# Narrowing w_out one block behind gate and val, and turning the second part of q two slots later, in a one-core attention and gated FFN kernel

## The chip, the cores and the metric

The kernel runs on one core of one Trainium2 chip. The metric is the device time of that core in microseconds. Before the change it is 303.82 us, the median of 10 runs that lie between 303.35 and 304.21 us. All times below are microseconds unless marked otherwise; the clock granted to TensorE is 1.0 over the whole span.

## What is computed

The reference is a linear attention with sketched features, followed by a gated feed-forward layer. Cut to what matters (B=4, H=4, S=1088, D=32, r=8, F=64; 4352 tokens, model width 128, inner width 1536):

```python
def phi(x):                      # S1, S2: (8, 32)
    a = einsum('rd,bhsd->bhsr', S1, x)
    b = einsum('rd,bhsd->bhsr', S2, x)
    return einsum('bhsi,bhsj->bhsij', a, b).reshape(..., 64)
kv  = einsum('bhsf,bhsd->bhfd', phi(k), v)
z   = sum(phi(k), axis=2)
x   = (phi(q) @ kv) / (phi(q) @ z + 1e-6)      # -> (4352, 128)
out = (sigmoid(x @ w_gate) * (x @ w_val)) @ w_out
```

S1, S2 and the three weight matrices arrive as 64-bit words. The kernel reads them as pairs of 32-bit integers and makes float32 of them itself; it calls that narrowing.

## The kernel before, in words

**The feed-forward part.** The 4352 tokens are cut into nine chunks of at most 512. For a chunk, the inner width is taken in 12 blocks j of 128. One *slot* (line 395) is one such block: `w1` (line 345) issues the gate and the val matmul of block j into a PSUM tile "wave" (128x512 each, line 357), ScalarE takes the sigmoid (line 365), and in the next slot VectorE multiplies the two (`glu`, line 381, tile g). Two slots after its `w1`, `w2` (line 314) multiplies g by block j of w_out and accumulates into the PSUM tile "moeout". So slot k issues glu(k-1), w2(k-2), w1(k), in this order. One float32 matmul of 512 columns shows in the trace as two instructions of about 0.43 us each, so a slot is six of these, 2.57 us of TensorE.

**The attention part.** Tokens of batch 0 must be ready before the first slot can run. The kernel makes the first 512 tokens (q part 0) in the prologue and starts slots at once; the other 576 tokens of batch 0 (q part 1) are made while the 12 slots of chunk 0 run. That goes in these steps: `turn_q(0, 1)` transposes q part 1 on VectorE (line 436); `q01` (line 1020) projects it on TensorE (tile cqps, line 602), ScalarE copies the result to SBUF (tile cq, line 610) and issues its DMA to DRAM (dq, line 620), and SyncE loads it back, spread over the partitions, with one DMA into qp and two into bq (line 627); `qmult(0, 1)` (line 655) multiplies qp by bq on VectorE; after that the denominators and numerators of q part 1 are matmuls (dps, line 841, and nps, line 861), and the division gives the tokens. qp of q part 1 is what dps reads. The SBUF buffer of bq is the one that held k and q of batch 0 and will hold those of batch 1, so `load_kq(1)` waits for `qmult(0, 1)`.

**The order around the change.** The program order of TensorE, VectorE, ScalarE and GpSimd is the order in which the Python code issues instructions; nothing reorders it. Before the change the order is: slot 0; slot 1; `turn_q(0, 1)`; slot 2; `q01`; slots 3 to 8; `qmult(0, 1)`; `load_kq(1)`; slot 9; then slot 10 with dps and nps in front of its matmuls; slot 11 with the last product; then chunk 1.

**Narrowing.** `narrow` (line 83) is a generator. Its step 0 clips the high words on GpSimd (cap, line 97) and scales the low words on ScalarE (tail, line 101); step 1 is two VectorE operations on the high words (head, lines 105 and 109); step 2 is a square on ScalarE (line 117), put in a PSUM bank or in place in SBUF, and an add on GpSimd (line 118); step 3 is the VectorE operation that writes the float32 weights to w_sb (line 127). The first two blocks are narrowed in three parts of 256 columns each (`narrow_01`): gate and val of block 0, gate and val of block 1, and w_out of blocks 0 and 1 together. Every later block j is one part of 384 columns: gate, val and w_out of the same j (`narrow_w`). The steps of these parts are issued inside `w1` of chunk 0, after the sigmoid (lines 366 to 376), a few slots ahead of their use. The weight loads are DMAs on SyncE's queue (lines 155 and 168), issued in the prologue in the order of their blocks.

Of the kernel before, what the change touches and what calls it, by code (L numbers as in the profile page):

```python
# [8 lines left out]
F32 = mybir.dt.float32  # L9
I32 = mybir.dt.int32  # L10
# [10 lines left out]
def kernel(  # L21
# [30 lines left out]
    const = ctx.enter_context(tc.tile_pool(name="const", bufs=1))  # L52
    ld = ctx.enter_context(tc.tile_pool(name="ld", bufs=1))
    sbA = ctx.enter_context(tc.tile_pool(name="sbA", bufs=2))
    raw = ctx.enter_context(tc.tile_pool(name="raw", bufs=NJ // 2))
    sbN = ctx.enter_context(tc.tile_pool(name="sbN", bufs=1))
    sbG = ctx.enter_context(tc.tile_pool(name="sbG", bufs=6))

# [24 lines left out]
    def narrow(out, bits, eng, bank=None, copies=None):  # L83

        p, n, m = bits.shape[:3]
        lo, hi = bits[:, :, :, 0].bitcast(U32), bits[:, :, :, 1]

        def tmp(dt, tag, bufs):
            return sbN.tile([P, 3, P], dt, tag=tag, name=tag, bufs=bufs)[:p, :n, :m]

        cap, tail = tmp(I32, "cap", 6), tmp(I32, "tail", 5)
        eng.tensor_scalar(  # L97
            out=cap.bitcast(F32), in0=hi.bitcast(F32), scalar1=122880.0, scalar2=-122880.0,
            op0=ALU.min, op1=ALU.max,
        )  # L100
        nc.scalar.activation(out=tail, in_=lo, func=ACTF.Copy, scale=2.0**-29)  # L101
        yield

        head = tmp(I32, "head", 3)
        nc.vector.tensor_scalar(
            out=head, in0=cap, scalar1=3, scalar2=0x3FFFFFF8,
            op0=ALU.logical_shift_left, op1=ALU.bitwise_and,
        )
        nc.vector.scalar_tensor_tensor(  # L109
            out=head, in0=cap, scalar=-0x40000000, in1=head, op0=ALU.bitwise_and, op1=ALU.bitwise_or  # L110
        )
        yield
        square = cap.bitcast(F32)
        if bank:
            square = pso.tile([P, 512], F32, tag=bank, name="square")[:, : n * m]
            square = square.rearrange("p (n m) -> p n m", n=n)
        nc.scalar.activation(out=square, in_=cap.bitcast(F32), func=ACTF.Square)  # L117
        nc.gpsimd.tensor_tensor(out=head, in0=head, in1=tail, op=ALU.add)  # L118
        yield

        head = head.bitcast(F32)
        if copies:
            square, head = (
                bass.AP(tensor=x.tensor, offset=x.offset, ap=[list(x.ap[0]), [0, copies], [1, m]])
                for x in (square, head)
            )
        nc.vector.scalar_tensor_tensor(  # L127
            out=out, in0=square, scalar=1.265625 * 2.0**-30, in1=head, op0=ALU.is_ge, op1=MUL
        )
        yield  # L130
# [11 lines left out]
                nc.sync.dma_start(out=rows, in_=s_)  # L142


    w_sb = const.tile([P, 3, NJ, P], F32, tag="w_sb", name="w_sb")
    w_in = {}

    def load_w_in(j0, j1):
        cs = slice(j0 * P, j1 * P)
        n, jj = divmod(j0, 2)  # L150
        if wide and jj == 0:
            w_in[n] = raw.tile([P, 3, 2, P, 2], I32, tag="w_in", name="w_in")
        for i, src in enumerate((moe_w_gate, moe_w_val)):
            if wide:
                nc.sync.dma_start(
                    out=w_in[n][:, i, jj : jj + j1 - j0].rearrange("p j m w -> p (j m w)"),
                    in_=src[:, cs].bitcast(I32),
                )
            else:
                nc.sync.dma_start(  # L160
                    out=w_sb[:, i, j0:j1].rearrange("p j m -> p (j m)"), in_=src[:, cs]
                )

    def load_w_out(n):
        j0, j1 = 2 * n, 2 * n + 2
        cs = slice(j0 * P, j1 * P)
        src = moe_w_out[cs, :].bitcast(I32) if wide else moe_w_out[cs, :]
        nc.sync.dma_start(
            out=w_in[n][:, 2].rearrange("p j m w -> p j (m w)") if wide else w_sb[:, 2, j0:j1],
            in_=src.rearrange("(j p) m -> p j m", p=P),  # L170
        )

    narrowing = {}

    def narrow_w(j, step):
        if not 0 <= j < NJ:
            return
        n, jj = divmod(j, 2)
        if wide:
            if step == 0:  # L180
                narrowing[j] = narrow(
                    w_sb[:, :, j, :], w_in[n][:, :, jj], nc.gpsimd, "acc1" if j < NJ - 2 else None
                )
            next(narrowing[j])


    def narrow_01(part, step):
        if wide:
            if step == 0:
                i = (slice(0, 2), part) if part < 2 else (2, slice(0, 2))  # L190
                narrowing["01", part] = narrow(
                    w_sb[:, i[0], i[1]],
                    w_in[0][:, i[0], i[1]],
                    nc.gpsimd,
                    "acc0" if part else "acc1",
                )
            next(narrowing["01", part])


    def load_rows(src, b, t, parts=((0, T, nc.sync),)):  # L200
# [42 lines left out]
    load_w_in(0, 1)  # L243
    v_t[0] = load_v(0)
    load_w_in(1, 2)
    load_w_out(0)
    load_rows(q, 0, q_t[0], ((T0, T, nc.sync),))
    for n in range(1, NJ // 2):
        load_w_in(2 * n, 2 * n + 2)
        load_w_out(n)  # L250


    def warm(*cols):
# [53 lines left out]
    def w2(ci, j0, jn, g):  # L307
# [4 lines left out]
        for jj in range(jn):  # L312
            j = j0 + jj
            nc.tensor.matmul(  # L314
                out=moe["acc"][:, :tw],
                lhsT=w_sb[:, 2, j, :],
                rhs=g[:, jj, :tw],
                start=(j == 0),
                stop=(j == NJ - 1),
            )  # L320
        if j0 + jn == NJ:
# [6 lines left out]
            while c < t0 + tw:  # L328
# [13 lines left out]
                    )  # L342
                c += n * 32

    def w1():

        ci = moe["ci"]
        t0, tw = tok_chk[ci]
        jn = TCH // tw
        j0 = moe["w"] * jn  # L350
        wv = psm.tile([P, 2, TCH], F32, tag="wave", name="wave")

        tp = tw // 2 if ci == 0 and j0 == 0 else tw
        for o in range(0, tw, tp):
            for which in range(2):
                for jj in range(jn):
                    nc.tensor.matmul(  # L357
                        out=wv[:, which, jj * tw + o : jj * tw + o + tp],
                        lhsT=w_sb[:, which, j0 + jj, :],
                        rhs=xT[:, t0 + o : t0 + o + tp],  # L360
                        start=True,
                        stop=True,
                    )
        sg = sbG.tile([P, TCH], F32, tag="sg", name="sg", bufs=3)
        nc.scalar.activation(out=sg, in_=wv[:, 0], func=ACTF.Sigmoid)  # L365
        if ci == 0:
            if j0 == 1:
                narrow_01(2, 3)
            if 0 < j0 < NJ - 2:
                narrow_w(j0 + 1, 3)  # L370
            narrow_w(j0 + 2, 1)
            narrow_w(j0 + 2, 2)
            if j0 < 3:
                narrow_w(j0 + 3, 0)
            if j0 > 1:
                narrow_w(j0 + 4, 0)


        def glu():
            g = sbG.tile([P, TCH], F32, tag="g", name="g")  # L380
            nc.vector.tensor_tensor(out=g, in0=wv[:, 1], in1=sg, op=MUL)  # L381
            moe["todo"].append((ci, j0, jn, g.rearrange("p (j t) -> p j t", j=jn)))

        moe["gate"] = glu
        moe["w"] += 1
        if j0 + jn == NJ:
            moe["ci"] += 1
            moe["w"] = 0
# [38 lines left out]
            in_=k_t[b][:, t0:t1].rearrange("p t d -> p (t d)"),  # L427
        )

    def turn_q(b, n):  # L430
        if b >= B:
            return
        if n == 0:
            qT_of[b] = sbA.tile([P, TP, 2, 32], F32, tag="qT", name="qT", bufs=1)
        t0, tn = q_chk[n]
        nc.vector.transpose(  # L436
            out=qT_of[b][:, t0 : t0 + tn].rearrange("p t c s -> p (t c s)"),
            in_=q_t[b][:, 2 * t0 : 2 * (t0 + tn)].rearrange("p t d -> p (t d)"),
# [211 lines left out]
                        in_=bass.AP(tensor=d0.tensor, offset=offset, ap=[[8 * W1, 32]] + run),  # L650
                    )

    def qmult(b, n):
        q0 = half(QP[b], n)
        nc.vector.tensor_tensor(out=q0, in0=q0, in1=half(BQ[b], n), op=MUL)  # L655

    def kv0(j_list):
        if 0 not in KVZ:
# [34 lines left out]
            )  # L693

    def kvd(b):
        KVD[b] = sbA.tile([P, 2, 2, F], F32, tag="kvd", name="kvd")
        k0 = KVZ[b][:, : 2 * F]
        n = 2 if b > 0 else 1
        nc.scalar.copy(
# [211 lines left out]

    if wide:
        steps = narrow(s4, s_in, nc.vector, copies=4)
        for _ in range(3):
            next(steps)
    turn_k(0, 0, KBASE[2] + 1)
    if wide:
# [51 lines left out]
    mult10 = ab(None, (0, 1, 0), (psm, "wave"))  # L969
    for pi in range(2):  # L970
        outer(0, pi, NJK - 1, NJK, eng=nc.gpsimd)
    for part in range(2):
        narrow_01(part, 0)
    spread_z()
    warm(512)
    for pi in range(2):
# [6 lines left out]
    def rest(turn, rc, dT):  # L983
# [5 lines left out]
        nt = rc.shape[1] - 1  # L989
        nc.scalar.activation(out=rc[:, :nt], in_=dT[:, :nt, :2], func=ACTF.Identity, bias=eps)  # L990
        kvd(0)
        narrow_01(0, 1)
        narrow_01(0, 2)
        ndt(0)

    divide = dn(0, 0, rest)
    warm(256)

    def head1():
        narrow_01(1, 1)  # L1000
        narrow_01(0, 3)
        narrow_01(1, 2)
        narrow_01(2, 0)
        narrow_w(2, 0)

    divide((0, 4), (4, 8), between=head1)
    narrow_01(1, 3)
    narrow_01(2, 1)
    narrow_01(2, 2)

    slot(None, 1)
    cq = {}
# [33 lines left out]
        kv(b, ZS[b])  # L1046
        kvd(b)

    slot(None, 1)
    turn_q(0, 1)  # L1050
    slot(None, 1)
    slot(q01, 6)
    qmult(0, 1)
    load_kq(1)
    slot(None, 1)
    slot(lambda: part01(lambda: narrow_w(NJ - 1, 3)), 1)
    slot(last01, 1)
    v_t[1] = load_v(1)
    for b in range(1, B):
# [60 lines left out]
```

## Time and profile before

| What | Value |
|---|---|
| profiled execution, its own time | 303.92 us |
| its span | 302.1 us |
| TensorE (PE) busy | 295.6 us, 1363 instructions |
| VectorE (DVE) busy | 154.8 us, 268 instructions |
| ScalarE (ACT) busy | 80.7 us |
| GpSimd (POOL) busy | 33.0 us |
| first matmul of slot 0 | 15.53 us |
| TensorE busy from 15.5 to 22.3 us | 6.46 of 6.80 us |
| TensorE busy from 22.3 to 45 us | 22.65 of 22.70 us |
| VectorE busy from 22.3 to 45 us | 18.48 of 22.70 us |

The span lacks 1.82 us of the execution's own time; that lies before its first and after its last instruction. A timeline row gives the start of a group, its length, the engine ("SPq" and "ACTq" are DMA issues by SyncE and ScalarE), the line, and what is written from what; a bracket at its end is the idle time of the engine ahead of it and who ended it. Rows of like instructions are merged with "xN". Ends of matmuls are modelled: a row of four 512-column matmuls is given as 1.88 us, while the next row starts 1.72 us after it.

### The profile page before, as it was taken

Reading aid. Unit: us, or ns where it says so; the run is one execution under the profiler, and the core shown is the slowest. Engines: PE = TensorE matmul, PEld = TensorE weight load, DVE = VectorE, ACT = ScalarE, POOL = GpSimd, SP = SyncE. Lnnn points to the kernel's source line nnn. Section 1 sums busy time; section 2 is a strip of 40 time slices with the busy share of each in tenths; the row PEclk is TensorE's granted clock in tenths of the full one; section 3 lists DMA queues with packets and bytes.
Section 4 is the critical chain, followed back from the end, with each engine's and each line's share of the span. In section 5 each row is a group of like instructions: output and inputs, shape, how many; then the busy total and the mean of one; then the engine's idle time right before and its main releaser. Section 6 shows DMA issues by size and latency. Waiting matters only on the chain.

```text
span 302.1 us, 3642 instructions
## 1 busy us (share of the span) xinstructions
PE 295.6 (98%) x1363; PEld 137.2 (45%) x1363; DVE 154.8 (51%) x268; ACT 80.7 (27%) x150; POOL 33.0 (11%) x62
## 2 busy tenths in 40 slices
PE   8899999999999999999999999999999999999994
PEld 3444434443444444544444445344444444444683
DVE  6998789774735554383365444932232223222331
ACT  3557523222122222212222222122222222222220
POOL 1365550410000400000004000000000000000000
PEclk9999999999999999999999999999999999999999
DMA  7993430796101491360017900200010000100011
GB/s 221 353 334 90 114 126 24 185 242 174 57 11 24 135 230 32 62 202 0 0 24 171 221 13 2 36 2 0 0 30 4 0 0 12 25 0 0 8 29 18
DMA packets 30546, 24.24 MB, mean 80 GB/s; under 512 B 20480, under 2 KB 25728, under 8 KB 30528
## 3 DMA queue, kind: packets, MB, share of 16 engines
q1 hardware_dynamic: 27024, 16.15, 20.4%
q0 software_dynamic: 2592, 7.08, 10.0%
q10 hardware_dynamic: 912, 0.77, 0.9%
q8 instruction: 11, 0.18, 0.3%
q14 instruction: 7, 0.06, 0.1%
HBM read 20.73 MB, written 3.26 MB: 79 GB/s over the span
## 4 chain that ended last, share of the span: by engine, by line
PE 84%; DMA 9%; DVE 3%; POOL 1%; SPq 1%; issue 1%; ACT 0%; DVEq 0%; POOLq 0%
PE wave L357 52%; PE moeout L314 27%; DMA w_in<-in_moe_w_out_dram 2%; DMA bq<-dq 2%; DMA v<-in_v_dram 2%; DMA w_in<-in_moe_w_val_dram 2%; DMA w_in<-in_moe_w_gate_dram 1%; PE nps L861 1%; POOL head L118 1%; PE kvz L677 1%; DVE qp L655 1%; PE kps L456 1%; DVE w_sb L127 1%; PE cqps L602 0%; PE deni L811 0%
## 5 line engine op out<-in xcount | busy, mean ns | idle before, releaser
L357 PE MATMUL wave<-xT,w_sb 128*128 128x512 f32 (+1 forms) x436 | 191.6, 565 | 0.0
L381 DVE TENSOR_TENSOR g<-wave,sg 128x512 f32<-128x512 f32 x102 | 70.3, 689 | 131.0 <-ACT sg L365 130.7
L357 PEld LDWEIGHTS wave<-xT,w_sb 128*128 128x128 f32 x436 | 82.7, 190 | 93.2 <-issue 86.0
L365 ACT ACTIVATE sg<-wave 128x512 f32<-128x512 f32 x102 | 60.9, 597 | 197.8 <-PE wave L357 197.8
L314 PE MATMUL moeout<-g,w_sb 128*128 128x512 f32 (+1 forms) x216 | 105.1, 574 | 0.3 <-DVE w_sb L127 0.3
L314 PEld LDWEIGHTS moeout<-g,w_sb 128*128 128x128 f32 x216 | 39.8, 190 | 44.8 <-issue 38.9
L118 POOL TENSOR_TENSOR head<-head,tail 128x384 int32<-128x384 int32 (+2 forms) x14 | 13.3, 952 | 17.9 <-DVE head L109 13.7
L627 POOL DMA_DIRECT2D qp<-dq x6 | 3.5, 583 | 106.2 <-DMA dq<-cq 106.2
L535 DVE TENSOR_TENSOR kp<-kab 128x1152 f32<-128x1152 f32 (+2 forms) x10 | 10.5, 1070 | 0.0
L655 DVE TENSOR_TENSOR qp<-qp,bq 128x1152 f32<-128x1152 f32 (+1 forms) x7 | 9.0, 1288 | 0.0
L258 PE MATMUL warm<-const-float32-1.0 128*128 128x512 f32 (+1 forms) x12 | 7.5, 755 | 0.8 <-PEq L1104 0.8
L109 DVE SCALAR_TENSOR_TENSOR head<-cap,head 128x384 int32<-128x384 int32 (+2 forms) x14 | 7.5, 534 | 0.5
L127 DVE SCALAR_TENSOR_TENSOR w_sb<-square,head 128x384 f32<-128x384 f32 (+1 forms) x11 | 5.7, 518 | 3.9 <-POOL head L118 3.9
L324 DVE STREAM_TRANSPOSE o_sb<-moeout 128x512 f32<-128x512 f32 (+1 forms) x9 | 6.1, 678 | 1.4 <-PE moeout L314 1.3
L627 POOL DMA_DIRECT2D bq<-dq x12 | 6.7, 575 | 0.5 <-issue 0.4
L101 ACT ACTIVATE tail<-w_in 128x384 int32<-128x384 uint32 (+1 forms) x13 | 6.5, 521 | 0.2 <-DMA w_in<-in_moe_w_gate_dram 0.2
L97 POOL TENSOR_SCALAR cap<-w_in 128x384 f32<-128x384 f32 (+1 forms) x13 | 6.4, 502 | 0.0
L886 DVE TENSOR_TENSOR xT<-nps,rb 128x576 f32<-128x576 f32 (+2 forms) x9 | 5.9, 659 | 0.5
L861 PE MATMUL nps<-qp,nd 64*32 64x256 f32 (+1 forms) x128 | 5.5, 401 | 0.5 <-ACT nd L741 0.4
L436 DVE STREAM_TRANSPOSE qT<-kq 128x512 f32<-128x512 f32 (+1 forms) x8 | 5.7, 718 | 0.0
L117 ACT ACTIVATE square<-cap 128x384 f32<-128x384 f32 (+1 forms) x11 | 5.1, 463 | 1.9 <-DVE w_sb L127 1.8
L425 DVE STREAM_TRANSPOSE kT<-kq 128x1088 f32<-128x1088 f32 (+2 forms) x5 | 5.4, 1072 | 0.2 <-DMA kq<-in_k_dram 0.2
(89 smaller groups left out, 85.8 us busy)
## 6 DMA issues: line engine op xcount, KB each, us to landing
qp<-dq POOLq DMA_DIRECT2D x6, 576.0 KB, 7.6
bq<-dq POOLq DMA_DIRECT2D x12, 288.0 KB, 9.4
v<-in_v_dram SPq DMA_DIRECT2D x16, 144.0 KB, 4.4
kq<-in_k_dram SPq DMA_DIRECT2D x3, 544.0 KB, 4.3
kq<-in_q_dram SPq DMA_DIRECT2D x3, 544.0 KB, 5.3
w_in<-in_moe_w_out_dram SPq DMA_DIRECT2D x6, 256.0 KB, 7.0
w_in<-in_moe_w_gate_dram SPq DMA_DIRECT2D x5, 256.0 KB, 6.2
w_in<-in_moe_w_val_dram SPq DMA_DIRECT2D x5, 256.0 KB, 6.5
```

Of the source, the lines that this page charges most:

```text
L109: nc.vector.scalar_tensor_tensor(out=head, in0=cap, scalar=-0x40000000, in1=head, op0=ALU.bitwise_and, op1=ALU.bitwise_or)
L118: nc.gpsimd.tensor_tensor(out=head, in0=head, in1=tail, op=ALU.add)
L127: nc.vector.scalar_tensor_tensor(out=out, in0=square, scalar=1.265625 * 2.0**-30, in1=head, op0=ALU.is_ge, op1=MUL)
L258: nc.tensor.matmul(out=t[:, 0, :n], lhsT=x, rhs=r, start=True, stop=True)
L314: nc.tensor.matmul(out=moe["acc"][:, :tw], lhsT=w_sb[:, 2, j, :], rhs=g[:, jj, :tw], start=(j == 0), stop=(j == NJ - 1),)
L357: nc.tensor.matmul(out=wv[:, which, jj * tw + o : jj * tw + o + tp], lhsT=w_sb[:, which, j0 + jj, :], rhs=xT[:, t0 + o : t0 + o + tp], sta ...
L365: nc.scalar.activation(out=sg, in_=wv[:, 0], func=ACTF.Sigmoid)
L381: nc.vector.tensor_tensor(out=g, in0=wv[:, 1], in1=sg, op=MUL)
L535: eng.tensor_tensor(out=KP[b][:, pi, j0:j1].rearrange("p j m (i l) -> p (j m) i l", i=R), in0=bass.AP(tensor=a0.tensor, offset=a0.offset, ...
L627: get.dma_start(out=t[64 * c : 64 * c + 64 if i else P, n * H * W1 : (n + 1) * H * W1], in_=bass.AP(tensor=d0.tensor, offset=d0.offset, ap ...
L655: nc.vector.tensor_tensor(out=q0, in0=q0, in1=half(BQ[b], n), op=MUL)
L861: nc.tensor.matmul(out=t[32 * h : 32 * h + 32, c, :w], lhsT=ND[b][rows, 32 * h : 32 * h + 32], rhs=half(QP[b], n)[rows, 2 * (h % 2) + h // ...
```

## The change

w_out is shifted by one block against gate and val. w_out 0 and w_out 1 are parts of their own (128 columns each); gate and val of blocks 0, 1 and 2 are parts of 256; from block 3 on a part holds gate and val of j with w_out of j - 1 (384 columns), and w_out 11 is a part of its own at the end. The raw tiles and w_sb are laid out for that, and w_out is loaded by eight DMAs where it was six. `narrow`'s step 1 is split in two (the two VectorE operations can be issued apart), so its steps are 0 to 4. The squares of w_out 1 and w_out 11 stay in SBUF. `turn_q(0, 1)` is cut in two pieces (5 and 4 of its 9 columns of tokens), issued in slots 3 and 4, and `q01` is issued ahead of slot 5. `qmult(0, 1)` stays behind slot 8. One buffer, kvd, has one copy where it had two. The core of the diff:

```diff
@@ narrow: two steps where there was one
             op0=ALU.logical_shift_left, op1=ALU.bitwise_and,
         )
+        yield
         nc.vector.scalar_tensor_tensor(
@@ parts
+    for j in range(NJ if wide else 0):
+        bits = w_in[j // 2][:, :, j % 2]
+        if j < 3:
+            at = slice(j, j + NJ + 1, NJ)
+            places["gv", j] = at, bits[:, :2], f"acc{1 - j % 2}"
+        else:
+            at = slice(j, j + 2 * NJ + 1, NJ)
+            places[j] = at, bits, "acc1" if j < NJ - 2 else None
+        for j, bank in enumerate(("acc0", None)):
+            places["out", j] = (
+                slice(2 * NJ + 1 + j, 2 * NJ + 2 + j), w_in[j][:, 2, 1 - j : 2 - j], bank
+            )
+        places[NJ] = slice(3 * NJ, 3 * NJ + 1), w_in[NJ // 2][:, 0], None
@@ loads
     load_w_in(1, 2)
-    load_w_out(0)
+    load_w_out(0, 1)
+    load_w_out(1, 2)
     load_rows(q, 0, q_t[0], ((T0, T, nc.sync),))
     for n in range(1, NJ // 2):
         load_w_in(2 * n, 2 * n + 2)
-        load_w_out(n)
+        if n == 1:
+            load_w_out(2, 3)
+        else:
+            load_w_out(2 * n - 1, 2 * n + 1)
+    load_w_out(NJ - 1, NJ)
@@ w1, chunk 0, after the sigmoid of block j0
-            if j0 == 1:
-                narrow_01(2, 3)
-            if 0 < j0 < NJ - 2:
-                narrow_w(j0 + 1, 3)
-            narrow_w(j0 + 2, 1)
-            narrow_w(j0 + 2, 2)
-            if j0 < 3:
-                narrow_w(j0 + 3, 0)
-            if j0 > 1:
-                narrow_w(j0 + 4, 0)
+            if j0 == 0:
+                narrow_w(("gv", 2), 1, 2, 3)
+                narrow_w(("out", 0), 4)
+                narrow_w(3, 0)
+            elif j0 == 1:
+                narrow_w(("gv", 2), 4)
+                narrow_w(("out", 1), 1, 2, 3)
+                narrow_w(3, 1, 2)
+                narrow_w(("out", 1), 4)
+                narrow_w(3, 3)
+                narrow_w(4, 0)
+            else:
+                if j0 in between:
+                    between[j0]()
+                if j0 != NJ - 2:
+                    narrow_w(j0 + 1, 4)
+                narrow_w(j0 + 2, 1, 2, 3)
+                if j0 <= 6:
+                    narrow_w(j0 + 3, 0)
+                if j0 >= 6:
+                    narrow_w(j0 + 4, 0)
@@ the prologue's last steps
     divide((0, 4), (4, 8), between=head1)
-    narrow_01(1, 3)
-    narrow_01(2, 1)
-    narrow_01(2, 2)
+    narrow_w(("gv", 1), 4)
+    narrow_w(("out", 0), 1, 2, 3)
@@ kvd
-        KVD[b] = sbA.tile([P, 2, 2, F], F32, tag="kvd", name="kvd")
+        KVD[b] = sbA.tile([P, 2, 2, F], F32, tag="kvd", name="kvd", bufs=1)
@@ the order
-    slot(None, 1)
-    turn_q(0, 1)
-    slot(None, 1)
-    slot(q01, 6)
+    between.update({3: lambda: turn_q(0, 1, 0, 5), 4: lambda: turn_q(0, 1, 5)})
+    slot(None, 4)
+    slot(q01, 4)
     qmult(0, 1)
     load_kq(1)
     slot(None, 1)
-    slot(lambda: part01(lambda: narrow_w(NJ - 1, 3)), 1)
+    slot(lambda: part01(lambda: narrow_w(NJ - 1, 4)), 1)
```

Slot 0 stands ahead of these lines in both kernels.

## Prediction

> **What bounds the kernel now.** I read the page first: busy time, then the chain that ended last. TensorE (PE) is busy 98% of the span, and the chain is mostly PE.
>
> ```profile
> PE 295.6 (98%) x1363; PEld 137.2 (45%) x1363; DVE 154.8 (51%) x268; ACT 80.7 (27%) x150; POOL 33.0 (11%) x62
> ...
> PE 84%; DMA 9%; DVE 3%; POOL 1%; SPq 1%; issue 1%; ACT 0%; DVEq 0%; POOLq 0%
> ```
>
> So the change is worth what it takes from, or adds to, PE's gaps between 15.5 us (slot 0) and 43 us (end of the q part 1 work). Behind that its order is unchanged. The timeline of PE shows the gaps:
>
> ```profile
> 15.53 3.71 PE L357 MATMUL wave<-xT,w_sb 128*128 128x256 f32 x12
> 19.58 1.12 PE L314 MATMUL moeout<-g,w_sb 128*128 128x512 f32 x2 [0.34 <-DVE w_sb L127]
> 20.54 1.88 PE L357 MATMUL wave<-xT,w_sb 128*128 128x512 f32 x4
> 22.35 0.69 PE L602 MATMUL cqps<-qT,skq 64*32 64x288 f32 x8
> 22.97 1.12 PE L314 MATMUL moeout<-g,w_sb 128*128 128x512 f32 x2
> ...
> 39.38 1.88 PE L357 MATMUL wave<-xT,w_sb 128*128 128x512 f32 x4
> 41.32 0.69 PE L841 MATMUL dps<-qp,zb 128*32 128x288 f32 x8
> ```
>
> Slots 0 and 1 stream 3.44 us of matmuls and are through at 18.97; the first w2 starts at 19.58. That is 0.61 us lost, not only the 0.34 in the bracket, since ends are modelled late. Wave 2 lost 0.10 (20.44 to 20.54). The other gap is at 41.32, 0.22 us behind wave 9. The timeline of VectorE (DVE) says who ends the first and the last:
>
> ```profile
> 18.52 0.68 DVE L381 TENSOR_TENSOR g<-wave,sg 128x512 f32<-128x512 f32 x1
> 19.12 0.41 DVE L127 SCALAR_TENSOR_TENSOR w_sb<-square,head 128x256 f32<-128x256 f32 x1
> ...
> 39.91 1.35 DVE L655 TENSOR_TENSOR qp<-qp,bq 128x1152 f32<-128x1152 f32 x1
> ```
>
> The first w2 waits for w_out 0/1, written at 19.12; dps waits for qmult, which ends at 41.27. Was qmult late for its data, or only for its turn on DVE? That is the question of this change, and SyncE's waits with the DMA shares by stretch answer it:
>
> ```profile
> SPq L202 <- DMA bq<-dq: 7.7, 1, 7.7
> SPq L202 <- DVE qp L655: 3.9, 1, 3.9
> ```
>
> ```profile
> 27.60:29.00 1.40, 1.40 (x4) 0.57 (x3) 0.87 (x3) 0.57 (x2) 0.96 (x2) 1.00 0.00 0
> 29.00:31.30 2.30, 2.30 (x7) 0.95 (x5) 1.70 (x4) 1.18 (x4) 1.49 (x2) 1.00 1.00 258
> 31.30:36.00 4.70, 4.70 (x13) 2.13 (x12) 3.43 (x8) 2.61 (x6) 2.57 (x4) 1.00 0.51 125
> 36.00:37.30 1.30, 1.30 (x5) 0.58 (x4) 1.27 (x4) 1.09 (x3) 0.42 (x1) 1.00 0.03 6
> ```
>
> SyncE issued qp at 27.62 and bq by 29.62, then waited 7.7 us for bq, to 37.3, and 3.9 us more for qmult. The last two columns of the stretches (DMA share, GB/s) agree: bytes move from 29.0 to 36.0. So the data was there 2.6 us before qmult's turn. The change moves exactly this chain later.
>
> **The early gain.** DVE's work up to the second xT product (15.86) is the same, so slot 0 starts at 15.53 again. Behind it DVE prepares w_out 0 as 128 columns, then gate/val 2 as 256, before glu(0). Start-to-start steps in the trace for 384/256 columns: L105 0.39/0.32, L109 0.48/0.34, L127 0.48/0.34. For 128 I extrapolate 0.25, 0.20, 0.20 (an estimate). From 16.54: w_out 0's two head operations to 16.99, gate/val 2's to 17.65; GpSimd's add for w_out 0 (0.72 for 256, 1.00 for 384, so about 0.44) runs from 17.2 to 17.65; w_out 0 is written by 17.98. glu(0) then waits only for its sigmoid (17.56 + 0.60 = 18.16) and ends at 18.86. The first w2 follows wave 1 at 18.97: minus 0.61. Gate/val 2 is written by 19.2, wave 2 needs it at 19.83: minus 0.10.
>
> In slots 1 and 2 the cover gets thin. L109 of block 3 starts at about 19.96, GpSimd's add ends 1.73 later (28.95 to 30.68 in a later slot), block 3 is written by 22.28 and wave 3 wants it at 22.4. A DVE-GpSimd round takes 2.62 us (28.09 to 30.71) against PE's 2.57, so wave 4 gets its weights at 24.90, and loading them takes 0.19. I charge PE 0.1 for both. Wave 4 then starts at 26.51 - 0.61 - 0.10 - 0.81 + 0.1 = 25.1; the 0.81 is cqps with its shape changes (23.93 less 22.26 and less the 0.86 of a w2), now behind wave 4.
>
> **Costed at nothing.** Six more DVE operations and two more parts on ScalarE and GpSimd: same elements, about 0.1 us each, beside PE, inside the 0.60 us per slot in which DVE waits for GpSimd's add; without that cover up to 0.6 on PE. The two pieces of turn_q (0.77 whole) in slots 3 and 4 lie in the same 0.60. Two more w_out DMAs on SyncE (0.38 to 0.43 each) put later weights, v of batch 1 and q part 1 behind them up to 0.9 later; block 6's weights had landed by 18.9 and were first used at 23.5, and q part 1, landed by 11.2, is now read at 23.7. A late block would cost PE us for us. Squares in SBUF: 0.52 against 0.49 on ScalarE. One kvd buffer: rewritten a batch after its last reader.
>
> **The late cost.** Wave 4 ends at 26.8; cqps follows; the sigmoid starts 0.22 behind the wave (28.23 to 28.43 later on), at 27.03. ScalarE's rows around the copy of cq before:
>
> ```profile
> 23.11 0.49 ACT L117 ACTIVATE square<-cap 128x384 f32<-128x384 f32 x1
> 23.54 1.01 ACT L101 ACTIVATE tail<-w_in 128x384 int32<-128x384 uint32 x2
> 24.57 0.63 ACT L610 COPY cq<-cqps 64x576 f32<-64x576 f32 x1
> 25.23 0.50 ACTq L620 DMA_DIRECT2D dq<-cq  x1
> ```
>
> After the change one tail stands before the copy, not two: sigmoid 0.50, square 0.41, tail 0.52, so cq is copied at 27.03 + 1.43 = 28.46, 3.89 later than 24.57. From there nothing is shorter: cq to qp's issue 3.05 (24.57 to 27.62), issue to bq landed 9.7. Data for qmult at 28.46 + 12.75 = 41.2. By order alone DVE could start qmult at 38.9 (block 9 written at 37.5, plus 1.33 as from 38.58 to 39.91). DVE is in order, so it now stands still for some 2.3 us; queued behind qmult are glu(8), the writing of block 10 and block 11's head operations. PE's wave 9 ends at 40.5 and dps stands next, w2(8) behind it.
>
> qmult takes 1.36 and dps starts 0.05 later: 42.6 against 41.32, that is +1.3. PE stands for 2.0 us, which eats the 0.71 of the early gain and more. All behind dps keeps its distance: load_kq(1) also waits for qmult; w_out 11's two head operations stand before glu(10), which I find at dps + 5.0 where it was + 4.9, against w2(10) at + 6.5.
>
> Bounds of the landing. The last byte moved at about 36.1. If it counts as landed as fast as dq did (last byte 27.2, next issue 27.62), data is there at 36.5, qmult starts at 40.4 and the loss is 0.5. SyncE's own wait says 37.3; I take that, since it is the row of these very transfers.
>
> **A rule against this row.** The Trainium skill, DMA: Bandwidth & Descriptors, section "Anatomy of one DMA", fits a GpSimd-issued DMA as 2.0 us plus its bytes over 436 GB/s. For the 1.18 MB of qp and bq that is 4.7 us (an estimate): landed at 31.5 + 4.7 = 36.2, no stall, and the early gain would stand. The row says 9.7, with half of the engines idle from 31.3 on. The measurement decides. Second, TensorE: Matmul & The Clock Gate, Part 1, has the clock fall to half after an idle window of some 3.4 us. No gap here is as long as 2.0 us, so no row tests it; by the rule nothing happens. If it fell for one such window, 1.7 us more.
>
> **Rivals.**
> - *The data comes in time* (faster). If the chain from cq to bq were 2.3 us shorter, DVE would take qmult at 38.9, dps would start at 40.6, right behind wave 9: minus 0.7, so 303.1 us. It decides where bq lands: before 38.9 full gain, at 39.9 break-even. For it: two bq DMAs overlap, and landing is inferred. Against: bytes still move at 36.0 in a stretch with no other traffic. Chance 0.12.
> - *Landing early in its bounds, or cq early*: a loss under 0.6, 303.5 to 304.4. Chance 0.17.
> - *The early gain fails as well*: if w_out 0 is again late (GpSimd's three clips before its add), cq and all behind it slip 0.6 more: 305.7. With a clock drop, 306.8. Chance 0.13 together.
> - *As costed*: chance 0.58.
>
> **How the numbers follow.** The profiled execution took 303.92 with a span of 302.1; it becomes 303.4 and 305.2. The median of the runs is 0.1 below that execution, so 305.1. The range leaves out the full gain and the clock drop: 303.6 to 306.1. A measurement here tells 0.2% (0.6 us) from no change: faster 0.12, same 0.17, slower 0.71.
>
> **What would show it.** Right: first w2 near 19.0; cq copied at 28.4 to 28.6; a gap of about 2 us before dps, its start near 42.6, and qmult starting within 0.1 of bq's landing with DVE idle before it. Wrong: qmult at about 39 (the landing was misread), first w2 still at 19.6, or a second gap behind dps from the crowded slots 9 to 12.

## The result and the profile after

The kernel after takes 305.45 us (median of 8 runs, 304.81 to 307.09), the one before 303.49 (29 runs, 303.23 to 307.46): a ratio of 1.007, 95% interval [1.0046, 1.0093]. That is slower by 2.0 us. The profiled execution of after took 307.66 us with a span of 305.8, that of before 303.92 with 302.1. The text below first takes this larger difference of 3.7 us apart.

The page of after, its busy times and the chain that ended last:

```profile
PE 297.3 (97%) x1363; PEld 137.5 (45%) x1363; DVE 155.7 (51%) x275; ACT 81.2 (27%) x154; POOL 32.7 (11%) x66
...
PE 89%; DMA 4%; DVE 3%; issue 2%; POOL 1%; ACT 1%; SPq 0%; DVEq 0%; POOLq 0%; ACTq 0%
```

As many matmuls as before keep PE busy 1.7 us longer (295.6 to 297.3): some of them ran slower. The rest must be gaps. PE's timeline shows both ("..." marks rows left out):

```profile
15.57 3.71 PE L374 MATMUL wave<-xT,w_sb 128*128 128x256 f32 x12
19.11 1.02 PE L329 MATMUL moeout<-g,w_sb 128*128 128x512 f32 x2
19.97 1.88 PE L374 MATMUL wave<-xT,w_sb 128*128 128x512 f32 x4
...
25.38 1.98 PE L374 MATMUL wave<-xT,w_sb 128*128 128x512 f32 x4
27.29 0.69 PE L632 MATMUL cqps<-qT,skq 64*32 64x288 f32 x8
...
39.17 1.88 PE L374 MATMUL wave<-xT,w_sb 128*128 128x512 f32 x4
43.32 0.69 PE L871 MATMUL dps<-qp,zb 128*32 128x288 f32 x8 [2.27 <-DVE qp L685]
43.95 1.21 PE L891 MATMUL nps<-qp,nd 64*32 64x288 f32 x16
45.09 2.07 PE L329 MATMUL moeout<-g,w_sb 128*128 128x512 f32 x2
46.95 2.09 PE L374 MATMUL wave<-xT,w_sb 128*128 128x512 f32 x4
48.88 1.02 PE L329 MATMUL moeout<-g,w_sb 128*128 128x512 f32 x2
```

The first w2 no longer waits (19.11, no bracket; it was 19.58 with 0.34). But dps, which waited 0.22 us behind wave 9, now has a bracket of 2.27 us that ends with qmult. Behind it the same groups take almost twice as long for a while: nps 1.21 us where it took 0.71, w2 2.07 where it takes 1.02 to 1.12, and then 1.02 again at 48.88. Who ended the gap is a row of VectorE's timeline:

```profile
39.27 0.56 DVE L110 SCALAR_TENSOR_TENSOR head<-cap,head 128x384 int32<-128x384 int32 x1
41.91 1.36 DVE L685 TENSOR_TENSOR qp<-qp,bq 128x1152 f32<-128x1152 f32 x1 [2.08 <-DMA bq<-dq]
```

VectorE is through with its earlier work at 39.8 and stands 2.08 us for bq; in before qmult followed the row above it without a bracket. The chain from the copy of cq to bq's issue, from the timeline of all engines:

```profile
29.07 0.63 ACT L640 COPY cq<-cqps 64x576 f32<-64x576 f32 x1
...
32.09 0.63 SPq L657 DMA_DIRECT2D qp<-dq  x1
...
32.81 1.26 SPq L657 DMA_DIRECT2D bq<-dq  x2
```

And the stretches of after (the last three columns are PE's granted clock, DMA share and GB/s):

```profile
33.00:36.00 3.00, 3.00 (x8) 1.33 (x7) 2.35 (x6) 1.98 (x5) 1.84 (x4) 1.00 0.81 203
36.00:40.00 4.00, 4.00 (x10) 1.67 (x9) 3.15 (x6) 2.07 (x5) 1.90 (x3) 1.00 0.51 124
40.00:41.90 1.90, 1.05 (x3) 0.19 (x1) 0.00 (x0) 1.25 (x3) 1.26 (x2) 1.00 0.17 43
...
43.30:44.00 0.70, 0.68 (x16) 0.21 (x21) 0.70 (x2) 0.00 (x0) 0.00 (x0) 0.96 0.00 0
44.00:47.20 3.20, 3.20 (x22) 1.25 (x20) 3.09 (x9) 0.52 (x1) 1.00 (x1) 0.50 0.88 297
47.20:55.00 7.80, 7.80 (x48) 3.21 (x47) 5.86 (x11) 2.00 (x4) 0.45 (x1) 0.99 0.05 21
```

Bytes of bq move at a DMA share of 0.51, half of the DMA engines, until about 40.6, just as they did some 4.5 us earlier in before. And from 44.0 to 47.2 PE's granted clock is 0.50; with the parts in the stretches on both sides (0.96 of 0.70 us, 0.99 of 7.80) the half clock lasts 3.4 us, and begins 0.6 us after dps has ended the gap.

To place the loss I measure from slot 0's first matmul, whose start shifts from run to run (14.9 to 15.7), to two later points: dps, and the first w2 behind the features of batch 1 ("features" below: 51.64 in before, 55.25 in after).

| | dps behind slot 0 | features behind slot 0 | features behind dps |
|---|---|---|---|
| before | 25.79 | 36.11 | 10.32 |
| after | 27.75 | 39.68 | 11.93 |

So +1.96 us to dps, +1.61 us from dps to the features (the half clock: 3.4 us at half speed would lose 1.7), together 3.57. The slot started 0.04 later, and behind the features the span is 0.1 us longer: that is the 3.7 us.

### The profile page after: what moved, and what is told of

Read it like the earlier page. It is cut to its first block, busy times and chain, and to the rows that moved or that the text cites. A ratio compares the mean times of both kernels' runs of the same rounds, so it can differ in the third digit from the quotient of the medians.

```text
span 305.8 us, 3668 instructions
## 1 busy us (share of the span) xinstructions
PE 297.3 (97%) x1363; PEld 137.5 (45%) x1363; DVE 155.7 (51%) x275; ACT 81.2 (27%) x154; POOL 32.7 (11%) x66
## 4 chain that ended last, share of the span: by engine, by line
PE 89%; DMA 4%; DVE 3%; issue 2%; POOL 1%; ACT 1%; SPq 0%; DVEq 0%; POOLq 0%; ACTq 0%
PE wave L374 54%; PE moeout L329 28%; DMA bq<-dq 3%; PE nps L891 2%; PE kvz L707 1%; DVE qp L685 1%; DMA s_in<-in_S_dram 1%; POOL head L119 1%; PE kps L486 1%; PE cqps L632 0%; PE deni L841 0%; PE dps L871 0%; PE kvz L693 0%; ACT sg L382 0%; DVE w_sb L128 0%
## 5 line engine op out<-in xcount | busy, mean ns | idle before, releaser
L329 PEld LDWEIGHTS moeout<-g,w_sb 128*128 128x128 f32 x216 | 39.9, 191 | 44.9 <-issue 38.9
L119 POOL TENSOR_TENSOR head<-head,tail 128x384 int32<-128x384 int32 (+3 forms) x16 | 12.8, 798 | 22.6 <-DVE head L110 16.2
L110 DVE SCALAR_TENSOR_TENSOR head<-cap,head 128x384 int32<-128x384 int32 (+3 forms) x16 | 7.8, 487 | 0.6
L128 DVE SCALAR_TENSOR_TENSOR w_sb<-square,head 128x384 f32<-128x384 f32 (+2 forms) x11 | 5.4, 495 | 3.3 <-POOL head L119 3.3
L101 ACT ACTIVATE tail<-w_in 128x384 int32<-128x384 uint32 (+2 forms) x15 | 6.8, 476 | 0.6 <-DMA w_in<-in_moe_w_out_dram 0.6
L97 POOL TENSOR_SCALAR cap<-w_in 128x384 f32<-128x384 f32 (+2 forms) x15 | 6.8, 463 | 0.0
L466 DVE STREAM_TRANSPOSE qT<-kq 128x512 f32<-128x512 f32 (+3 forms) x9 | 5.8, 654 | 0.0
L105 DVE TENSOR_SCALAR head<-cap 128x384 int32<-128x384 int32 (+3 forms) x16 | 5.3, 332 | 0.0
```

Source lines behind the costliest of these rows:

```text
L97: eng.tensor_scalar(out=cap.bitcast(F32), in0=hi.bitcast(F32), scalar1=122880.0, scalar2=-122880.0, op0=ALU.min, op1=ALU.max,)
L110: nc.vector.scalar_tensor_tensor(out=head, in0=cap, scalar=-0x40000000, in1=head, op0=ALU.bitwise_and, op1=ALU.bitwise_or)
L329: nc.tensor.matmul(out=moe["acc"][:, :tw], lhsT=w_sb[:, 2 * NJ + 1 + j, :], rhs=g[:, jj, :tw], start=(j == 0), stop=(j == NJ - 1),)
```

## The experiments

Theory: **the late q chain**. cq copied 3.9 us or more later makes bq land later than VectorE's turn for qmult, and PE stands. Rivals: the new narrowing costs the time by itself (crowded slots); or the loss is mostly the clock. Times are medians in us, and each ratio is against runs of before on the same chip. The last three columns come from the one profiled execution of each kernel and are measured as in the table above.

| kernel | us | ratio, 95% interval | dps behind slot 0 | features behind slot 0 | features behind dps |
|---|---|---|---|---|---|
| after, again | 305.37 | 1.0068 [1.0038, 1.0098] | 27.29 | 37.69 | 10.40 |
| before's narrowing, after's q order | 305.66 | 1.009 [1.0058, 1.0123] | 27.68 | 38.01 | 10.33 |
| after's narrowing, before's q order | 304.40 | 1.0025 [1.0017, 1.0033] | 25.69 | 36.61 | 10.92 |
| after, q ahead of slot 4 | 304.05 | 1.002 [1.0012, 1.0028] | 25.59 | 36.50 | 10.91 |
| after, bq on all DMA engines | 303.79 | 1.001 [1.0004, 1.0017] | 25.56 | 36.49 | 10.93 |
| after, gap filled | 305.64 | 1.0062 [1.0045, 1.008] | 27.13 | 37.45 | 10.32 |
| before's q order, w_out 11 early | 304.15 | 1.0023 [1.0014, 1.0033] | 26.35 | 36.67 | 10.32 |
| q in slots 2 and 3, w_out 11 early | 304.14 | 1.0024 [1.0015, 1.0032] | 26.24 | 36.56 | 10.32 |
| q ahead of slot 4, reordered | 304.76 | 1.0037 [1.0024, 1.0049] | 26.78 | 37.10 | 10.32 |
| q in slots 2 and 3, w_out 11 early, reordered | 306.16 | 1.0079 [1.0066, 1.0092] | 27.83 | 38.16 | 10.33 |
| before, reordered | 304.74 | 1.0039 [1.0026, 1.0052] | 26.99 | 37.31 | 10.32 |
| q in slots 2 and 3, reordered from slot 4 | 304.91 | 1.0037 [1.0024, 1.0051] | 26.65 | 36.97 | 10.32 |

**The two halves of the change, one at a time.** After's narrowing with before's order of q:

```diff
-    between.update({3: lambda: turn_q(0, 1, 0, 5), 4: lambda: turn_q(0, 1, 5)})
-    slot(None, 4)
-    slot(q01, 4)
+    slot(None, 1)
+    turn_q(0, 1)
+    slot(None, 1)
+    slot(q01, 6)
```

> The changed narrowing alone: q part 1 is turned after slot 1 and projected ahead of slot 3, as in the kernel before. My theory (the late q chain makes the loss): bq lands by 37.5 us, VectorE never waits for it, dps starts between 41.2 and 41.7 us, the time is 303.2 to 303.9 us, within 0.2% of before, and TensorE's clock stays at 1.0. Rival (the new narrowing costs the time, by its crowded slots and two more weight DMAs): 305 us or more, dps at 43 us.

and before's narrowing with the three removed lines of this diff in place of its own order:

> The kernel before with only the q steps moved: turned in two pieces in slots 3 and 4, projected ahead of slot 5. My theory: the first w2 still starts at 19.6 us; cq is copied near 29.3 us, bq lands 12.8 us later near 42.1, VectorE waits about 2 us for it, dps starts at 43.5 us: 305.3 to 305.8 us with the clock at 1.0, 1.6 us more where it falls to a half behind the gap. Rival (the narrowing costs the time): 303.5 us, as before.

The second takes 305.66 us, as its theory expected: the q order alone loses as much as the whole change. Its VectorE row at qmult has the same bracket as after's:

```profile
41.58 1.36 DVE L660 TENSOR_TENSOR qp<-qp,bq 128x1152 f32<-128x1152 f32 x1 [1.78 <-DMA bq<-dq]
```

The first has no such bracket; qmult comes by its order behind L110, and dps 0.1 sooner than in before:

```profile
39.51 0.56 DVE L110 SCALAR_TENSOR_TENSOR head<-cap,head 128x384 int32<-128x384 int32 x1
39.98 1.35 DVE L685 TENSOR_TENSOR qp<-qp,bq 128x1152 f32<-128x1152 f32 x1
```

Yet at 304.40 us it lies above its expected range, 0.9 us slower than before. Of the 0.6 us won ahead of the first w2 only 0.1 is left at dps, and 0.6 us are lost between dps and the features. PE's timeline shows where:

```profile
50.58 0.72 PE L486 MATMUL kps<-kT,sk 64*32 64x288 f32 x16
51.66 0.72 PE L632 MATMUL cqps<-qT,skq 64*32 64x288 f32 x16 [0.37 <-DVE qT L466]
```

cqps of batch 1 follows kps by 1.08 us; in before it is 0.51 (50.51, 51.02). It waits for VectorE's turning of batch 1's q, which starts 34.47 us behind slot 0 where it was 33.81. The three operations for w_out 11, which before does not have as operations of their own, take VectorE 0.63 us ahead of it. So there is a second cost, and it is the narrowing's. In after it doesn't show, since VectorE had caught up while PE stood ahead of dps.

**How long the q chain may be.** The transposes whole in slot 3, q01 one slot earlier:

```diff
-    between.update({3: lambda: turn_q(0, 1, 0, 5), 4: lambda: turn_q(0, 1, 5)})
-    slot(None, 4)
-    slot(q01, 4)
+    between.update({3: lambda: turn_q(0, 1)})
+    slot(None, 3)
+    slot(q01, 5)
```

> The changed kernel with the q steps one slot earlier: q part 1 turned whole in slot 3, projected ahead of slot 4. My theory: cq near 26.5 us, bq landed near 39.3, before VectorE reaches qmult in its own order (39.7 us); no wait for data; dps near 41.1 us, 0.2 us earlier than before, 303.2 us. Rival (the narrowing costs the time): 305 us. If the landing depends on something else than cq's time, dps stays behind 42 us.

One slot (2.6 us) is enough: qmult has no bracket, and dps comes 0.2 us sooner than in before, as expected. But the kernel takes 304.05 us and not the expected 303.2: cqps of batch 1 waits for qT here too (0.35 us). The other way is to leave q where after has it and to make bq land sooner. bq is read by two DMAs over 64 partitions each, at the share of 0.51; here one DMA over all 128 partitions reads 16 rows of dq, so bq's contents (and what is computed from them) are not the reference's:

```diff
+                if b == 0 and i:
+                    get.dma_start(
+                        out=t[:, n * H * W1 : (n + 1) * H * W1],
+                        in_=bass.AP(..., ap=[[8 * W1, 2 * R], [0, R], [1, H * W1]]),
+                    )
+                    continue
```

> The changed kernel, but bq of q part 1 is loaded by one DMA over 128 partitions that reads 16 rows, each 8 times, as qp's does, in place of two over 64 partitions that read 8 rows each; bytes and order are the same, the contents of bq are not the reference's. If the 9.7 us from issue to landing come from the half of the DMA engines that bq uses, the bytes now move at a DMA share near 1.0 and end about 2.4 us sooner after qp's issue: bq lands near 39.5 us, VectorE's wait goes, dps starts near 41.2, the time is 304.0 to 304.5 us. Rival (a fixed latency or DRAM sets the landing): it lands at 41.5 or later again, 305 us.

It takes 303.79 us, 0.2 less than the expected range. Its stretches, to be held against the 0.51 of after between 36 and 40:

```profile
33.00:36.00 3.00, 3.00 (x8) 1.33 (x7) 2.35 (x5) 2.34 (x6) 1.99 (x3) 1.00 1.01 249
36.00:38.00 2.00, 2.00 (x6) 0.91 (x5) 1.36 (x4) 0.92 (x3) 1.11 (x2) 1.00 0.94 217
38.00:39.00 1.00, 1.00 (x4) 0.39 (x3) 0.97 (x3) 0.60 (x1) 0.39 (x1) 1.00 0.01 0
```

The share stays near 1 and the bytes end at 38. SyncE's wait for bq, 6.1 us from the end of its issue at 32.9, gives a landing at 39.0: 10.4 us behind the copy of cq (28.60), where it was 12.8 in the first profile of after and 12.4 in the second, whose run lay beside this one. With that the gap ahead of dps is gone. An earlier start and a faster transfer each remove it, so the late q chain is shown to be its cause.

**The clock.** After again, and after with two 512-column matmuls of constants written into dps's bank ahead of dps, which fill the gap:

```diff
+        for _ in range(2 if b == 0 and n == 1 else 0):
+            ones = nc.const_aps.tensor(1.0, [P, P], F32)
+            nc.tensor.matmul(
+                out=dps, lhsT=ones, rhs=nc.const_aps.tensor(1.0, [P, TCH], F32), start=True, stop=True
+            )
```

> The changed kernel once more, as it is, for its landing time and its clock on the chip of these runs: two groups of runs, near 305.2 us with the mean clock at 1.0 and near 307 us at 0.994; where the profile has the clock at 1.0, nothing but the wait ahead of dps differs from before.

> The changed kernel with two 512-column float32 matmuls of ones, 1.7 us, written to the dps bank just ahead of dps: they lie in TensorE's gap of 2.3 us and move nothing else. If the runs near 307 us come from the clock that falls to a half behind that gap, all runs are now near 305.2 us with the clock at 1.0, and dps still starts at 43.3 us. Rival (the slow group has another cause): runs fall in two groups again, near 305.2 and 307.0 us.

The second profile of after has a gap of 1.81 us at the same place and no slow matmuls behind it:

```profile
42.95 0.69 PE L871 MATMUL dps<-qp,zb 128*32 128x288 f32 x8 [1.81 <-DVE qp L685]
43.57 0.71 PE L891 MATMUL nps<-qp,nd 64*32 64x288 f32 x16
```

Of the 14 executions of after, 5 have a mean clock of 0.994 and take 306.85 to 307.66 us; the other 9 have 0.998 to 1.0 and take 304.62 to 305.75 (median 305.16). The kernel with before's narrowing and after's order has 1 of its 4 at 0.994 (308.08). The one with the gap filled has none in 6, and the nine other kernels, which have no such gap, have none at 0.994 in 88; nor has before in the 84 whose clock is on record. Two executions without the gap were long as well: one with q ahead of slot 4 (0.983, 309.0 us) and one of before (307.46 us, its clock not on record). So the gap need not be the only cause. PE's rows with the gap filled:

```profile
40.20 1.89 PE L872 MATMUL dps<-const-float32-1.0 128*128 128x512 f32 x4
42.02 0.69 PE L880 MATMUL dps<-qp,zb 128*32 128x288 f32 x8
```

That run came out other than expected: its times lie between 304.66 and 306.27 us, not all near 305.2, and dps starts at 42.02, not 43.3. Slot 0 began at 14.89, and bq landed 11.9 us behind cq, so that VectorE stood for only 1.15 us.

So the half clock goes with the gap (6 of 18 executions with it), and costs 1.9 us between the two medians of after (307.09 and 305.16), 1.6 in the trace. It is not the main loss: the executions without it are still 1.7 us above before, and with the gap filled the median is no lower (305.64). Whether the fall depends on the gap's length (2.27 us with, 1.81 without) or on something else, two profiles can't say, and 6 runs are few for the filled gap. Where the gap lies may count too: in the trace of after the clock became full at 6.40, fell at 43.94 and came back at 47.36, so the fall stands 11 times the 3.41 us of the half clock behind 6.40. Of the 3.41 us before the fall TensorE stood for about 2.4; in the second profile of after (full at 6.58) the eleventh such stretch ends at 44.13, TensorE stood for about 2.0 of it, and the clock stayed. That it goes by such stretches is a reading of these traces, not shown.

**The narrowing's own cost.** If the 0.6 us behind dps come from w_out 11, whose three VectorE operations stand in slots 10 to 12 ahead of batch 1's transposes, narrowing it in slots 4 to 6 must bring them back; once with before's q order, once with the transposes in slots 2 and 3 (the conditions that keep the other steps as they were are left out here):

```diff
+                if j0 == 5:
+                    narrow_w(NJ, 1, 2, 3)
+                if j0 == 6:
+                    narrow_w(NJ, 4)
...
+                if j0 == 4:
+                    narrow_w(NJ, 0)
```

> The changed narrowing with the q order of the kernel before, as in the first experiment, and w_out 11 narrowed in slots 4 to 6 where VectorE waits for GpSimd, not in slots 8 to 12. Theory of the second loss (w_out 11's head operations and write push the transposes of batch 1 back, and cqps of batch 1 waits for qT): the wait of TensorE on qT near 51 us goes, 0.5 us less than the first experiment: 303.7 to 304.0 us. Rival (the rest is elsewhere): 304.4 us again.

> A candidate: the changed narrowing, q part 1 turned in two pieces in slots 2 and 3 and projected ahead of slot 4, w_out 11 narrowed in slots 4 to 6. From the third experiment's trace: cqps no longer waits 0.4 us for the turn, no wait for bq, no wait of cqps of batch 1: dps 25.2 us behind the first matmul of slot 0 (25.8 before, 25.6 in the third experiment), 303.0 us, or 303.4 if only the second gap goes.

Both missed, at 304.15 and 304.14 us. The wait of cqps is gone (10.32 from dps to the features, as before), so w_out 11's place was its cause. But dps comes 0.45 to 0.56 us later than in before. PE's rows of the second:

```profile
33.98 1.88 PE L374 MATMUL wave<-xT,w_sb 128*128 128x512 f32 x4
...
36.74 1.98 PE L374 MATMUL wave<-xT,w_sb 128*128 128x512 f32 x4
...
39.73 1.99 PE L374 MATMUL wave<-xT,w_sb 128*128 128x512 f32 x4
```

From wave to wave it is 2.76 and 2.99 where PE alone takes 2.575. The cost only moved. In all five variants with the new narrowing, q in time and the old order of a slot's steps, cqps of batch 1 comes 35.84 to 36.05 us behind slot 0; in before 35.49.

Where the early gain goes can be read in the variant with bq on all engines, which has no gap ahead of dps. It is 0.61 us ahead of before at wave 2 and 0.25 at wave 9. Waves 3 and 4 start 2.74 and 2.67 us behind the wave ahead, 0.26 in all over PE's own 2.575, and the slot with cqps is 0.1 longer (3.49 for 3.39). After has the same steps, and in its trace the weight loads for waves 3 and 4 (at 22.70 and 25.37) each end a wait of 0.66 us for w_sb.

The round between VectorE and GpSimd was my explanation for the late weights: w_sb written, two head operations, GpSimd's addition, w_sb written again, 2.67 us (after: 27.42, 30.09, 32.76), against PE's 2.575. The two more weight DMAs are a rival that was not tested apart; from 15 to 45 us the variant has one wait for a weight DMA, 0.6 us of GpSimd, where before has none. Three kernels try to break the round by letting the next block's head operations go first; the same edit in before's lines is the third:

```diff
-                if j0 != NJ - 2:
-                    narrow_w(j0 + 1, 4)
-                narrow_w(j0 + 2, 1, 2, 3)
+                narrow_w(j0 + 2, 1, 2)
+                if j0 != NJ - 2:
+                    narrow_w(j0 + 1, 4)
+                narrow_w(j0 + 2, 3)
```

> The kernel with q ahead of slot 4, and from slot 2 on the two head operations of block j0 + 2 stand ahead of the writing of block j0 + 1, so that GpSimd's addition for j0 + 2 runs beside that writing and glu, not between them. Theory (what is left of the early gain is taken by the round of VectorE and GpSimd, 2.67 us against TensorE's slot of 2.575): VectorE's idle time of about 0.5 us ahead of each w_sb write is gone, the small waits of TensorE in slots 6 to 9 are gone, dps comes 25.1 to 25.4 us behind slot 0's first matmul where it came 25.6, and the time is about 303.7 us; the wait of batch 1's cqps for qT behind the third features stays (0.35 us). Rival (TensorE's own order and qmult's turn set dps): dps stays at 25.6 and the time at 304.05.

> The kernel with q in slots 2 and 3 and w_out 11 narrowed in slots 4 to 6, with the same reordering as the other kernel of this call. Theory (the round is what made the early w_out 11 as dear as the late one): without the round VectorE has some 0.4 us to spare in each slot, so neither slots 7 to 9 nor batch 1's cqps wait; dps at 25.1 to 25.4 us behind slot 0, the features of batch 1 about 35.6 behind it where before had 36.11 and the kernel without the reordering 36.56; the time is 303.0 us, below before by 0.5. Rival (VectorE's work as such is too much[...]): waits in slots 7 to 9 stay, 303.8 to 304.2.

> The kernel before with this reordering alone (head operations of block j0 + 2 ahead of the writing of block j0 + 1). Theory: before lost nothing to the round in its slots but 0.22 us ahead of dps, where qmult came 0.7 late for its turn; with the round broken qmult comes earlier and the gap goes: 303.3 us, within 0.1% of before. Rival (before's slots hold hidden losses to the round, too): 302.9 or less. Either way its 0.6 us ahead of the first w2 stays.

All three are slower than theory or rival had it, before's too. In the first, VectorE's rows:

```profile
22.48 0.36 DVE L105 TENSOR_SCALAR head<-cap 128x384 int32<-128x384 int32 x1 [0.90 <-POOL cap L97]
22.87 0.56 DVE L110 SCALAR_TENSOR_TENSOR head<-cap,head 128x384 int32<-128x384 int32 x1
23.35 0.55 DVE L128 SCALAR_TENSOR_TENSOR w_sb<-square,head 128x384 f32<-128x384 f32 x1
```

and PE's row behind them:

```profile
23.95 1.98 PE L374 MATMUL wave<-xT,w_sb 128*128 128x512 f32 x4 [1.20 <-DVE w_sb L128]
```

The head operations now come first, but their cap isn't there: GpSimd clips it only behind its previous addition. The weights that wave 3 needs were ready to be written and stand queued behind that wait: 1.2 us of PE. From wave 4 to wave 8 the same kernel keeps 2.575 a slot (27.45, 30.02, 32.60, 35.17, 37.75), so only the first slot seemed to cost. (In the second kernel waves 7 and 8 wait again, 0.42 and 0.20 us, each for w_sb.) The last kernel therefore reorders from slot 4 on:

```diff
+                if j0 > 3:
+                    narrow_w(j0 + 2, 1, 2)
                 if j0 != NJ - 2:
                     narrow_w(j0 + 1, 4)
-                narrow_w(j0 + 2, 1, 2, 3)
+                if j0 < 4:
+                    narrow_w(j0 + 2, 1, 2)
+                narrow_w(j0 + 2, 3)
```

> The kernel after with the two pieces of turn_q in slots 2 and 3, q01 ahead of slot 4, and the head operations of block j0 + 2 ahead of the writing of block j0 + 1 from slot 4 on only; w_out 11 stays where the kernel after has it. Theory (the reordering cost the earlier three only in its first slot, where the cap of the next block was not there yet and weights for a wave came 1.2 us late; its later slots kept TensorE's pitch): no wait ahead of waves 3 and 4, cqps at 9.05 behind slot 0, wave 4 at 10.65 behind it, then 2.575 a slot, so dps at 25.3 and the features of batch 1 at 35.6 to 35.8 where before had 36.11: 303.1 to 303.4 us, below before by 0.1 to 0.4. Rival (the reordering shifts other work, or what it lets overlap is stretched, so that the first slots were not its only price): the features at 36.3 or later, 303.9 us or more.

It missed as well: 304.91 us and the features at 36.97, on the rival's side. Its first slots are as wished (cqps 9.05 behind slot 0, wave 4 at 10.63), then VectorE stands in slot after slot:

```profile
27.45 0.36 DVE L105 TENSOR_SCALAR head<-cap 128x384 int32<-128x384 int32 x1 [1.10 <-POOL cap L97]
...
32.80 0.36 DVE L105 TENSOR_SCALAR head<-cap 128x384 int32<-128x384 int32 x1 [0.54 <-POOL cap L97]
```

The slot between these two waits in the same way (30.12, 0.65 us). The one round was exchanged for another: addition (1.00), the next cap on GpSimd (0.53), two head operations, addition again, 2.67 us a time once more. By this reading the caps would have to run a block earlier as well; that was not tried. No version here beats the kernel before.

## Why the prediction was right

The cause was right: the q chain moved by more than its slack, VectorE stood for bq, and TensorE stood behind it. The time (305.1 predicted, 305.45 measured) is closer than the sum behind it, and that is partly luck. The prediction put 1.3 us on top of 303.82. Measured were 1.96 on top of 303.49, or 1.67 in the executions at full clock, so the lower median of before took back half of what was missing in the rise. And three of the eight runs of after carry the half clock, which the prediction had left out. Term by term:

- *Slot 0 at 15.53 again; the first w2 0.61 earlier, wave 2 another 0.10.* Right: 15.57, and from slot 0 to the first w2 3.54 us where it was 4.05, to wave 2 4.40 where it was 5.01. The 0.61 and the 0.10 came as 0.51 and 0.10.
- *Thin cover in slots 1 to 4, charged 0.1 us.* Too little: PE's pitch from wave 2 to wave 4 is 2.74 and 2.67, which is 0.26 over its own. The round of VectorE and GpSimd took 2.67, not 2.62. With the 0.10 missing above, wave 4 stands 9.81 behind slot 0; predicted was 9.57.
- *cq copied at 28.46.* It was 29.07. Measured from slot 0 that is 0.57 more: 0.24 of wave 4, 0.14 to the start of the sigmoid, 0.19 from there to the copy. This is the mis-sized term of the sum: it makes dps +1.96 instead of +1.3. So the chain's head moved by 4.5 us, not by 3.9.
- *12.75 us from cq to qmult; qmult by its turn at 38.9; dps 1.4 behind qmult.* 12.84, 39.8 and 1.41. The turn was 0.9 later than costed, which did not matter, since the data came later still. SyncE's wait was read rightly, and for this run the earlier reading (data at 36.5, loss 0.5) is ruled out. But 12.84 is one execution: the same steps took 12.4 us in the second profile of after, 12.1 with before's narrowing and 11.9 with the gap filled. That the landing hit to 0.1 us is partly luck, and the loss at dps goes with it (+1.50 in the second profile).
- *By the fit of the Trainium skill (DMA: Bandwidth & Descriptors, "Anatomy of one DMA"), which is for DMAs that GpSimd issues, 1.18 MB land 4.7 us after the issue (an estimate), with no stall.* The row won: 9.8 us in after. With one DMA over all partitions for bq it was 7.4 us (31.6 to 39.0), still behind the fit.
- *No clock fall by the rule of the Trainium skill (TensorE: Matmul & The Clock Gate, Part 1).* Wrong. The prediction's gap of 2.0 us was held for harmless against an idle window of some 3.4 us; at 2.27 the clock fell in the profiled execution, and in 5 of 14. The price, put at 1.7 us, was 1.6 in the trace. It was left out of the range, and it is why the highest runs (307.09) lie outside.
- *Six more VectorE operations costed at nothing; w_out 11 before glu(10), and "no second gap".* Wrong as a statement on the kernel, right for this one run, and by luck: the gap ahead of dps hid it. With q in time it costs some 0.6 us behind dps (or, put elsewhere, 0.5 ahead of it). The wrong-sign rival, that the data in time gives 303.1 us, falls with it: with bq in time the kernel takes 303.79 to 304.40, not less than before.
- *Everything behind dps keeps its distance.* Without the half clock it does: 10.40 in the second profile of after, 10.32 in before.

The 0.6 us won at the first w2 were real; at most 0.23 of them reached dps in any variant, and the wait for qT took more than that. That waves 3 and 4 wait for their weights, and that w_out 11's operations make cqps of batch 1 wait, is shown. That the round of VectorE and GpSimd is what makes the weights late is argued from the 2.67 us; the attempts to break the round only built another, so it is not shown.

With before's q order the median lies 0.9 us above before, while the profile loses 0.5 from slot 0 to the features. Another 0.17 is a later slot 0 (15.70 for 15.53), which shifts from run to run by more than that; the rest stays open.

## What to carry to other kernels

When an edit moves the head of a chain that crosses DMAs, add up the chain to its last consumer from the rows of those very transfers, and compare it with the consumer's turn in its own queue: here the slack was 2.6 us, the move 4.5, and an early gain of 0.6 could not pay for it. Leave room for the spread of such a chain, too: in four traces with the same transfers the steps took 11.9 to 12.8 us. A gain ahead of a run of slots can be lost again in these slots, as here in waves 3 and 4, so check that the engines that prepare their data can follow before counting it. And a stall of the bound engine hides smaller costs of the same edit, so undo the parts one at a time before calling any of them free.

## What the runs showed of the hardware

TensorE's granted clock fell to 0.50 for 3.4 us after an idle gap of 2.27 us, and stayed at 1.00 after one of 1.81 us at the same place. The 0.59 MB of bq in two DMAs, at a DMA share of 0.51, landed 9.4 and 9.8 us behind the issue of qp in the two profiles of after; in one DMA over all partitions, at 0.94 to 1.01, they landed 7.4 us behind it.

Where VectorE's qmult and GpSimd's addition overlap, the one that starts second takes longer. In after they do not overlap, and qmult takes 1.36 us and the addition 1.00. In before qmult starts 0.26 us ahead (39.91) and keeps its 1.35, while the addition takes 1.96:

```profile
40.17 1.96 POOL L118 TENSOR_TENSOR head<-head,tail 128x384 int32<-128x384 int32 x1 [1.13 <-DVE head L109]
```

In the last kernel the addition starts first and keeps its 1.00; qmult takes 2.00, and the clip of 128 columns that starts during qmult takes 1.40 (0.30 in after):

```profile
39.12 1.00 POOL L119 TENSOR_TENSOR head<-head,tail 128x384 int32<-128x384 int32 x1 [0.59 <-DVE head L110]
39.34 2.00 DVE L689 TENSOR_TENSOR qp<-qp,bq 128x1152 f32<-128x1152 f32 x1
...
40.09 1.40 POOL L97 TENSOR_SCALAR cap<-w_in 128x128 f32<-128x128 f32 x1
```

Six traces have the first order and four the second, and all ten agree. So the reordering also made qmult longer, by up to 0.65 us.
